# A planner rule that mixes FFN products into attention, with junk products ahead of it, in a fused mLSTM and two-FFN kernel

## The chip, the cores and the metric

The kernel runs on one NeuronCore of a Trainium2 chip. The metric is the device time of one execution in microseconds (us). TensorE (PE in the profile) multiplies, VectorE (DVE), ScalarE (ACT) and GpSimd (POOL) do the elementwise work, and SyncE (SP) issues the DMA transfers.

## What is computed

A recurrent attention with gates (an mLSTM) over 4 batches, 8 heads, 768 steps and 40 values per head, and behind it two feed-forward networks (FFNs) on the 3072 x 320 result:

```python
for t in range(S):                                   # per batch and head
    m_new = np.maximum(f_gate[t] + m, i_gate[t])
    f_stab, i_stab = np.exp(f_gate[t] + m - m_new), np.exp(i_gate[t] - m_new)
    C = f_stab * C + i_stab * outer(v[t], k[t]);  n = f_stab * n + i_stab * k[t]
    y[t] = sigmoid(o_gate[t]) * (C @ q[t]) / np.maximum(abs(n @ q[t]), 1.0);  m = m_new
x = y.transpose(0, 2, 1, 3).reshape(B * S, H * D)
x = np.maximum(np.maximum(x @ w1, x @ w2), x @ w3) @ w_out        # 320 -> 768 -> 320
h = x @ w_in                                                      # 320 -> 2048
out = (h * np.clip(h + 3.0, 0.0, 6.0) / 6.0) @ w_out2             # 2048 -> 320
```

## The kernel before

The recurrence is cut into 6 chunks of 128 steps. A group `g` (0 to 23) is one chunk of one batch, with its 8 heads; it is written out in `attention(g)`. Within a group TensorE runs these steps, each of 8 to 16 or 32 small instructions: `bc` (lines 407 to 412, groups 0 to 3 only) broadcasts a gate row; `sc` (450, two steps a group) multiplies keys and queries; `in` (471) multiplies queries with the state of the chunk before; `pv` (484) sums the values; `dc` (547) makes the new state; `tr` (521) transposes the result for the FFN. `gps` (310) transposes gate values. In the first two chunks (groups 0 to 7) `sc` and `in` multiply on 40 rows in f32, later on 120 rows in a split format. DVE, ACT and POOL work between these steps: a decay scan and a product for `fd`, sums, a reciprocal, the sigmoid.

The first FFN takes blocks of 2, 2, 4, 4, 4, 4 and 4 groups (`BLK1`), so its products are 256 columns wide for two blocks and 512 later. A step `h` (`f_in`, line 630) is 8 products of one of six slices `k` with one of three weights; ACT or DVE takes the running maximum `m`; ACT and POOL split it into `hh`; a step `acc` (`f_out`, line 663) is 5 or 3 products that sum the outputs over the slices. Each of the 24 weight tiles arrives as raw 64-bit data and passes through ACT, DVE, ACT (line 609) and POOL in `weights(k, p)`. The second FFN (from line 763; `pi`, `po`) follows in the same way and is not touched.

What runs when on each engine in the first part is written out by a planner, `class Plan`. Every step is entered by `P.add` with an engine, a cost in ns, a priority `pr` (lower comes first; attention has 1000 times its group, FFN products 10**6 and more), what it reads and writes, and so its buffers (`BUFS`: three PSUM buffers `pa` for `sc`, `in`, `pv`, `dc`, `tr`, `gps`; two `h`; and so on). Steps of FFN products carry the tag `ffn`. `order()` is a list scheduler: in each round it works out for every ready step the earliest start `s` (its engine, its inputs with a latency, a free buffer), and takes the step with the smallest key; so the earliest start wins, and the priority decides between equal starts. The loop at line 748 then issues the steps in the planned order of start; each engine keeps that order. Where the plan leaves TensorE over 600 ns without work, the loop puts in products of constant data (`wps`, line 751), counted at 430 ns each on a running clock `t_pe`, until the first step that uses the PSUM buffer `acc2`, which `wps` shares.

Of the kernel before, what the change touches and what calls it, by code (L numbers as in the profile page):

```python
# [33 lines left out]
JOIN, LAG1 = 4, 3  # L34
BLK2 = [4] * 6
LAG, PIB = 3, 5
SLOPE = 0.0
AHEAD, WPR = 5, 100
GPB, GGB = 3, 4
PE_, PM, PC = 0, 2 * 10**6, 3 * 10**6  # L40
NM1, NM2 = max(BLK1) * L, max(BLK2) * L
# [36 lines left out]
class Plan:  # L78
# [22 lines left out]
    def order(p):  # L101
        free = {t: [0.0] * b for t, b in BUFS.items()}
        left = {s: len(u) for s, u in p.users.items()}
        ends = {s: 0.0 for s in p.users}
        live, done = set(), {}
        at = dict.fromkeys(("PE", "DVE", "ACT", "POOL", "SP"), 0.0)
        dma = 0.0
        todo = {o["n"]: len(o["deps"]) for o in p.ops}
        after = {}
        for o in p.ops:  # L110
            for d in o["deps"]:
                after.setdefault(d, []).append(o["n"])
        ready = {n for n, k in todo.items() if k == 0}
        res = []
        while ready:
            best = None
            for n in ready:
                o = p.ops[n]
                s = at[o["eng"]]
                for d in o["deps"]:  # L120
                    x = p.ops[d]
                    end = done[d]
                    if x["eng"] != o["eng"] or x["eng"] == "SP":
                        end += p.LAT.get(x["eng"], 0) + o["wait"]
                    s = max(s, end)
                ok = True
                for t in o["slots"] - live:
                    if not free[t[0]]:
                        ok = False
                        break  # L130
                    s = max(s, min(free[t[0]]) + 100)
                if ok:
                    e = at[o["eng"]]
                    s = max(s, e)
                    key = (s + SLOPE * min(o["pr"], 20000), o["pr"], n, s)
                    if best is None or key < best:
                        best = key
            assert best, "no buffer for any step"
            _, _, n, s = best
            o = p.ops[n]  # L140
            ready.discard(n)
            for t in o["slots"] - live:
                free[t[0]].remove(min(free[t[0]]))
                live.add(t)
            o["at"] = s
            at[o["eng"]] = s + o["ns"]
            end = s + o["ns"]
            if o["eng"] == "SP":
                dma = max(dma, s) + o["size"] / 210
                end = dma + 2000  # L150
            done[n] = end
            for t in o["slots"]:
                left[t] -= 1
                ends[t] = max(ends[t], end)
                if left[t] == 0:
                    free[t[0]].append(ends[t])
            res.append(o)
            for m in after.get(n, ()):
                todo[m] -= 1
                if todo[m] == 0:  # L160
                    ready.add(m)
        assert len(res) == len(p.ops), "a step never comes"
        p.end = max(done.values())
        return sorted(res, key=lambda o: (o["at"], o["n"]))


def body(tc, ctx, qk0, qkf, kvo, ig, fg, w1, w2, out):
    nc = tc.nc
# [14 lines left out]
    def prio(p):  # L183
        tc.cur_priority = p
# [39 lines left out]
    def products(ps, wt, hi, lo, x):  # L224
        order = [(hi, 0), (hi + 128, 1), (lo, 0), (hi, 3), (lo + 128, 1), (hi + 128, 4), (hi + 256, 2), (lo + 256, 2)]
        for n, (a, r) in enumerate(order):
            nc.tensor.matmul(ps, wt[:, a:a + 128], x[:, r], start=n == 0, stop=n == len(order) - 1)  # L227
# [5 lines left out]
    with ExitStack() as c1:  # L233
# [3 lines left out]
        late = {}  # L237
# [12 lines left out]
        junk = cs1.tile([128, 512], BF16, name="junk")  # L250
# [485 lines left out]
        for seq, (what, j, k) in enumerate(order1()):  # L736
# [3 lines left out]
            else:  # L740
                f_out(j, k, 4 * seq)
        order = P.order()
        n_gates = max(n for n, o in enumerate(order) if o["tags"] & {"gf", "gi", "gm"})

        wps = psh.tile([128, 512], F32, tag="acc2", name="wps")
        t_pe, fill = 500.0, True
        with tc.manual_schedule():
            for n, o in enumerate(order):
                if o["eng"] == "PE" and fill:
                    while n and t_pe + 600 < o["at"]:  # L750
                        nc.tensor.matmul(wps, junk[:, 0:128], junk, start=True, stop=True)  # L751
                        t_pe += 430
                    t_pe = max(t_pe, o["at"]) + o["ns"]
                if n == n_gates + 1:
                    gp1.__exit__(None, None, None)
                    late["hp"] = c1.enter_context(pool("hp"))
                if "acc2" in o["tags"]:
                    fill = False
                prio(10 * n)
                o["fn"]()  # L760


    with ExitStack() as c2:
# [131 lines left out]
def build(arrays):  # L895
    nc = bacc.Bacc("TRN2", target_bir_lowering=False, num_devices=1)
    args = {
        n: nc.dram_tensor(f"in_{n}", a.shape, mybir.dt.from_np(a.dtype), kind="ExternalInput").ap()
        for n, a in arrays.items()
    }  # L900
    out = nc.dram_tensor("out_0", (B * S, DM), F32, kind="ExternalOutput").ap()
    with tile.TileContext(nc, schedule_with_timeline_sim=True) as tc, ExitStack() as ctx:
        body(tc, ctx, out=out, **args)
    return nc
# [9 lines left out]
```

## Time and profile before

| | us |
|---|---|
| median of 3 runs | 808.36 (807.01 to 811.66) |
| the profiled execution | 809.83 |
| its span, first to last instruction | 808.1 |
| TensorE busy | 792.9 (98%) |
| POOL, DVE, ACT busy | 372.3, 351.3, 308.9 |

The table is read from the top: the metric, then the one execution that the profile shows, then the share of its span in which each engine worked. The busy time counts an engine at work and says nothing of its speed. TensorE's clock has two levels, and the profile gives the granted clock beside the busy times, as a part of full speed.

### The profile page before, as it was taken

The numbers are of one execution on the slowest core, as the hardware profiler recorded it, in microseconds if no ns is written. First come the engines' busy times: TensorE is split into PE (matmuls) and PEld (weight loads), VectorE is DVE, ScalarE is ACT, GpSimd is POOL, SyncE is SP. The second block draws the span as 40 slices with busy tenths as digits, with TensorE's granted clock in tenths as the row PEclk, the third lists the DMA queues.
The fourth block names the chain that finished last, engine by engine and source line by source line (L and its number), as shares of the span: only waits on it lengthen the run. The fifth ranks groups of instructions, "written<-read, shape, count | busy, mean of one in ns | idle before, by whom it ended". The sixth has DMA issues, their size and how long they took to land.

```text
span 808.1 us, 12015 instructions
## 1 busy us (share of the span) xinstructions
PE 792.9 (98%) x4583; PEld 698.7 (86%) x4585; DVE 351.3 (43%) x562; ACT 308.9 (38%) x594; POOL 372.3 (46%) x338
## 2 busy tenths in 40 slices
PE   9999999999999998999999999999999999999997
PEld 7789999988888786888788888899898988989886
DVE  5658555766557454564423666321212212121110
ACT  2645351213222221321422889443434333443432
POOL 2557664664756544432411556533534434343332
PEclk7557788999999998999999999999999999999999
DMA  7677576766776736841421454100200000000000
GB/s 221 119 212 259 185 242 178 192 185 171 215 229 212 222 117 176 219 171 49 133 66 34 151 176 136 51 16 1 66 1 1 33 1 1 34 1 1 33 1 33
DMA packets 48974, 91.77 MB, mean 114 GB/s; under 512 B 5740, under 2 KB 25748, under 8 KB 48596
## 3 DMA queue, kind: packets, MB, share of 16 engines
q1 hardware_dynamic: 48916, 91.00, 38.3%
q8 instruction: 36, 0.59, 0.3%
q14 instruction: 22, 0.18, 0.1%
HBM read 70.81 MB, written 18.45 MB: 110 GB/s over the span
## 4 chain that ended last, share of the span: by engine, by line
PE 85%; ACT 5%; POOL 3%; DVE 3%; DMA 2%; issue 1%; SPq 1%; ACTq 0%; POOLq 0%
PE h L227 22%; PE pi L227 19%; PE po L836 6%; PE po L835 6%; PE po L837 6%; PE pv L487 6%; PE sc L453 5%; PE acc L674 5%; PE in L474 3%; PE dc L550 2%; PE acc L676 2%; PE bc L412 1%; DVE t L210 1%; DMA qs<-qs_d 1%; PE wps L751 1%
## 5 line engine op out<-in xcount | busy, mean ns | idle before, releaser
L227 PE MATMUL h<-x,w 128*128 128x512 f32 (+1 forms) x1008 | 227.9, 380 | 1.1 <-ACT m L642 1.1
L821 POOL TENSOR_TENSOR gg<-r,gg 128x512 fp32r<-128x512 f32 x96 | 125.6, 1317 | 183.5 <-ACT gg L820 173.4
L227 PEld LDWEIGHTS h<-x,w 128*128 128x128 f32 x1008 | 180.3, 205 | 31.7 <-ACT m L642 2.5
L227 PE MATMUL pi<-xs,w 128*128 128x512 f32 x768 | 193.3, 395 | 1.5 <-ACT w L779 0.8
L227 PEld LDWEIGHTS pi<-xs,w 128*128 128x128 f32 x768 | 140.8, 188 | 29.7 <-ACT w L779 1.1
L818 DVE SCALAR_TENSOR_TENSOR r<-r,pi 128x512 f32<-128x512 f32 x96 | 64.3, 686 | 229.4 <-ACT r L817 229.2
L835 PE MATMUL po<-w,gg 128*128 128x320 f32 x384 | 118.2, 310 | 0.5 <-DVE x L704 0.2
L836 PE MATMUL po<-w,gg 128*128 128x320 f32 x384 | 118.0, 309 | 0.0
L817 ACT ACTIVATE r<-pi,b 128x512 f32<-128x512 f32 x96 | 63.8, 685 | 133.9 <-PE pi L227 133.3
L837 PE MATMUL po<-w,gg 128*128 128x320 f32 x384 | 111.2, 309 | 0.0
L658 POOL TENSOR_TENSOR hh<-m,hh 128x512 fp32r<-128x512 f32 (+1 forms) x42 | 51.1, 1217 | 89.3 <-ACT hh L654 80.0
L644 DVE TENSOR_TENSOR m<-h,m 128x512 f32<-128x512 f32 (+1 forms) x84 | 51.4, 612 | 87.4 <-PE h L227 82.7
L835 PEld LDWEIGHTS po<-w,gg 128*128 128x128 f32 x384 | 72.1, 188 | 4.8 <-ACT gg L820 0.6
L674 PE MATMUL acc<-hh,w 128*128 128x512 f32 (+1 forms) x252 | 75.1, 376 | 0.0
L836 PEld LDWEIGHTS po<-w,gg 128*128 128x128 f32 x384 | 72.1, 188 | 3.1
L820 ACT CAST gg<-r 128x512 fp32r<-128x512 f32 x96 | 59.0, 621 | 36.6 <-DVE r L818 34.4
L654 ACT CAST hh<-m 128x512 fp32r<-128x512 f32 (+1 forms) x42 | 23.5, 559 | 128.5 <-PE acc L674 124.6
L837 PEld LDWEIGHTS po<-w,gg 128*128 128x128 f32 x384 | 70.4, 188 | 0.9
L217 POOL TENSOR_TENSOR w<-t,w 128x384 fp32r<-128x384 f32 (+2 forms) x46 | 43.6, 961 | 27.2 <-ACT w L609 15.4
L427 DVE TENSOR_TENSOR_SCAN fd<-fd,ident 128x512 f32<-128x512 f32 x40 | 51.6, 1297 | 2.8 <-DMA fd<-f_d 2.7
L674 PEld LDWEIGHTS acc<-hh,w 128*128 128x128 f32 x252 | 46.1, 195 | 6.9
L487 PEld LDWEIGHTS pv<-vt,fd 128*128 128x128 f32 x384 | 50.5, 209 | 1.4 <-issue 0.4
(83 smaller groups left out, 859.2 us busy)
## 6 DMA issues: line engine op xcount, KB each, us to landing
raw<-in_w SPq DMA_DIRECT2D x34, 384.0 KB
kvo<-in_kvo SPq DMA_DIRECT2D x24, 488.0 KB
fd<-f_d SPq DMA_DIRECT2D x20, 512.0 KB
qs_d<-sp SPq DMA_DIRECT2D x16, 640.0 KB
qs<-qs_d SPq DMA_DIRECT2D x64, 160.0 KB
raw<-in_w SPq DMA_DIRECT2D x22, 320.0 KB
raw<-in_qkf SPq DMA_DIRECT2D x16, 320.0 KB
qs<-qs_d SPq DMA_DIRECT2D x16, 320.0 KB
```

The lines of the kernel that those rows point to most:

```text
L227: nc.tensor.matmul(ps, wt[:, a:a + 128], x[:, r], start=n == 0, stop=n == len(order) - 1)
L427: nc.vector.tensor_tensor_scan(out=half, data0=s.get(("bc", a), half), data1=ident4.rearrange("p h t -> p (h t)"), initial=0.0, op0=ALU.mu ...
L487: nc.tensor.matmul(ps[:, h], s["fd"][:, h], s["vt"][:, h], start=True, stop=True)
L644: nc.vector.tensor_tensor(out=T["m", j, k], in0=T["h", j, k, w], in1=T["m", j, k], op=ALU.max)
L674: nc.tensor.matmul(acc[a], wo[:, a * 128:128 + a * 128], h, start=first, stop=last)
L817: nc.scalar.activation(r, ps, AF.Relu, bias=b3)
L818: nc.vector.scalar_tensor_tensor(out=r, in0=r, scalar=6.0, in1=ps, op0=ALU.min, op1=ALU.mult)
L820: nc.scalar.copy(gg[:, 0], r)
L821: nc.gpsimd.tensor_tensor(out=gg[:, 1], in0=r, in1=gg[:, 0].bitcast(F32), op=ALU.subtract)
L835: nc.tensor.matmul(po[t], hi, wo[:, 0:320], start=first, stop=False)
L836: nc.tensor.matmul(po[t], hi, wo[:, 320:640], start=False, stop=False)
L837: nc.tensor.matmul(po[t], lo, wo[:, 0:320], start=False, stop=last)
```

## The change

A constant `RUN = 1000, 800` is added and `SLOPE`, which was 0.0, goes. In the planner, `low` counts the ns of TensorE steps planned since the last one that was tagged `ffn`. While it is over 1000, the key of every TensorE step without that tag is its start plus 800 ns. The start itself is not changed. Each kind of buffer gets a ranked list of its users (by the priority of the first step that uses each), and where only one buffer of a kind is free, no step gets it but the one whose tile is first in rank. In the loop that issues the steps, each TensorE step is followed by round(ns/900) products of constant data, 128 x 512 in bf16, counted at 215 ns each on `t_pe`; and filling ends at the first step that carries `acc2` or `ffn`.

```diff
-SLOPE = 0.0
+RUN = 1000, 800
...
+        live, done, rank = set(), {}, {}
+        for t, u in p.users.items():
+            rank.setdefault(t[0], []).append(((p.ops[min(u)]["pr"], min(u)), t))
+        for x in rank.values():
+            x.sort()
...
                 for t in o["slots"] - live:
-                    if not free[t[0]]:
+                    if not free[t[0]] or len(free[t[0]]) == 1 and t != rank[t[0]][0][1]:
                         ok = False
                         break
...
-                    key = (s + SLOPE * min(o["pr"], 20000), o["pr"], n, s)
+                    late = RUN[1] if o["eng"] == "PE" and "ffn" not in o["tags"] and low > RUN[0] else 0
+                    key = (s + late, o["pr"], n, s)
...
                 live.add(t)
+                rank[t[0]] = [x for x in rank[t[0]] if x[1] != t]
+            if o["eng"] == "PE":
+                low = 0.0 if "ffn" in o["tags"] else low + o["ns"]
...
-                if "acc2" in o["tags"]:
+                if o["tags"] & {"acc2", "ffn"}:
                     fill = False
                 prio(10 * n)
                 o["fn"]()
+                if o["eng"] == "PE" and fill:
+                    for _ in range(round(o["ns"] / 900)):
+                        nc.tensor.matmul(wps, junk[:, 0:128], junk, start=True, stop=True)
+                        t_pe += 215
```

## Rows read from the trace of the kernel before

**Rows 1.** Page, part 1: busy us, share of span, instructions of each engine.
```profile
PE 792.9 (98%) x4583; PEld 698.7 (86%) x4585; DVE 351.3 (43%) x562; ACT 308.9 (38%) x594; POOL 372.3 (46%) x338
```

**Rows 2.** Page, part 2: granted TensorE clock in 40 slices, tenths.
```profile
PEclk7557788999999998999999999999999999999999
```

**Rows 3.** Windows: length, busy us (count) by engine, clock, DMA, GB/s.
```profile
9.10:33.00 23.90, 23.57 (x116) 19.43 (x116) 15.74 (x23) 10.22 (x20) 8.96 (x12) 0.50 0.66 191
33.00:52.30 19.30, 19.08 (x106) 17.06 (x107) 8.66 (x20) 11.64 (x30) 8.68 (x12) 0.59 0.87 183
52.30:141.00 88.70, 88.45 (x641) 84.92 (x641) 54.45 (x100) 37.22 (x87) 55.85 (x64) 0.78 0.67 211
141.00:300.00 159.00, 157.44 (x1040) 137.31 (x1040) 97.95 (x164) 40.37 (x79) 91.49 (x87) 1.00 0.66 194
300.00:341.00 41.00, 37.58 (x201) 31.43 (x200) 19.38 (x32) 9.11 (x17) 20.18 (x18) 0.92 0.74 196
```

**Rows 4.** TensorE groups up to 52.3 us: count | busy us, mean ns.
```profile
L453 PE MATMUL sc<-qs 40*128 40x128 f32 x56 | 13.3, 427 | 0.0
L412 PE MATMUL bc<-gf,ident 32*128 32x128 f32 x64 | 13.2, 373 | 0.3 <-DVE fd L427 0.3
L487 PE MATMUL pv<-vt,fd 128*128 128x42 f32 x48 | 9.3, 375 | 0.0
...
L550 PE MATMUL dc<-vw,kvo 128*40 128x42 f32 x48 | 4.0, 276 | 0.0
...
L314 PE MATMUL gps<-ident,gi 32*128 32x32 f32 x6 | 1.3, 240 | 0.0
```

**Rows 5.** TensorE's timeline, first stretch: start us, us, operation, instructions.
```profile
15.78 3.64 PE L487 MATMUL pv<-vt,fd 128*128 128x42 f32 x16
19.35 3.78 PE L453 MATMUL sc<-qs 40*128 40x128 f32 x16
...
28.44 4.47 PE L751 MATMUL wps<-junk 128*128 128x512 bf16 x10 [0.33 <-issue]
```

**Rows 6.** Timeline, the same kinds of product later.
```profile
119.57 1.07 PE L227 MATMUL h<-x,w 128*128 128x256 f32 x8
...
139.53 1.87 PE L487 MATMUL pv<-vt,fd 128*128 128x42 f32 x16
```

**Rows 7.** Windows before and after the clock's fall at 73.9 us.
```profile
63.70:73.90 10.20, 10.20 (x105) 9.74 (x106) 7.42 (x15) 6.52 (x16) 6.91 (x7) 1.00 0.83 289
73.90:87.60 13.70, 13.70 (x60) 12.80 (x60) 9.93 (x14) 6.57 (x16) 11.08 (x12) 0.50 0.81 257
```

**Rows 8.** Timeline: the row ending in this fall, FFN product behind.
```profile
67.83 2.05 PE L453 MATMUL sc<-qs 40*128 40x128 f32 x16
...
70.56 1.98 PE L474 MATMUL in<-cn,qs 40*128 40x42 f32 x16
...
72.85 2.56 PE L487 MATMUL pv<-vt,fd 128*128 128x42 f32 x16
75.20 2.05 PE L227 MATMUL h<-x,w 128*128 128x256 f32 x8
```

**Rows 9.** Timeline: first and last of an attention row after 141 us.
```profile
245.09 0.97 PE L474 MATMUL in<-cs,qs 120*128 120x42 f32 x8
...
247.79 1.43 PE L550 MATMUL dc<-vw,kvo 128*40 128x42 f32 x32
```

**Rows 10.** Timeline, TensorE's longest wait.
```profile
311.15 1.94 PE L453 MATMUL sc<-qs 120*128 120x128 f32 x8 [3.15 <-DMA qs<-qs_d]
```

**Rows 11.** TensorE's waits for FFN buffers: us in total, times, longest.
```profile
PE h L227 <- ACT m L642: 1.1, 2, 0.7
```

**Rows 12.** Line 609, weight casts: count, durations, first and last start.
```profile
L609 ACT CAST w<-t x24: 445/512/525, 19.8 to 109.2; 128x384 fp32r<-128x384 f32 x18, 128x320 fp32r<-128x320 f32 x6
```

**Rows 13.** Timeline: last attention product, and FFN products behind it.
```profile
382.48 0.49 PE L524 MATMUL tr<-ident,y 128*128 128x128 f32 x3
...
418.48 5.66 PE L227 MATMUL h<-x,w 128*128 128x512 f32 x24
```

More of the change, by code (lines that the diff above doesn't have):

```diff
@@ L104, in order @@
         ends = {s: 0.0 for s in p.users}
-        live, done = set(), {}
+        live, done, rank = set(), {}, {}
[3 more added lines that the diff above has]
+            x.sort()
         at = dict.fromkeys(("PE", "DVE", "ACT", "POOL", "SP"), 0.0)
-        dma = 0.0
+        dma = low = 0.0
         todo = {o["n"]: len(o["deps"]) for o in p.ops}
```

## The prediction

> **What bounds the kernel now.** I read the busy shares first. TensorE is busy 792.9 of 808.1 us [rows 1], and no other engine reaches half: what ends last is TensorE's own stream, so a change pays only if it shortens that stream. The share hides one thing, which stands a few lines below it on the page: the granted clock, at half in early slices and full from about 140 us on [rows 2]. The windows by stage put numbers on it [rows 3]. From 9.1 to 33 us TensorE is busy 23.57 of 23.90 us at a clock of 0.50, to 52.3 us 19.08 of 19.30 at 0.59, to 141 us 88.45 of 88.70 at 0.78; from 141 to 300 the clock is 1.00. As the clock has two levels (1.2 and 2.4 GHz), a mean of 0.78 over 88.7 us is 2 x 0.22 x 88.7 = 39.0 us at half. In the same way the first two stretches hold 23.9 + 15.8 = 39.7 us, and the 41 us from 300 on (0.92) 6.6 us. Some 85 us run at half clock, and they are the reserve that this change can touch.
>
> What the same product costs at each level is in the timeline. A `pv` step takes 3.64 us early and 1.87 at full clock, a pair of `sc` steps 3.78 and 2.05, eight `h` products of 256 columns 2.05 and 1.07 [rows 5, 6, 8]. A step at full clock takes about 0.55 of its time at half, so a microsecond at half gives back at most 0.45 us. All of it together: 85.3 x 0.45 = 38 us.
>
> What TensorE did before the clock fell: from 67.83 to 75.20 us it ran only attention products (`sc`, `dc`, `in`, `tr`, `pv`), 7.4 us in a row [rows 8], and the clock, full to 73.9, is at half from there to 87.6 [rows 7]. Three more such rows, of 4.5, 4.4 and 4.0 us, end in a fall between 89 and 127 us. After 141 us, where FFN products are mostly 512 columns wide and `in` and `sc` work on 120 rows in place of 40, even a row of 4.1 us (`in`, `pv`, `dc`) costs no clock [rows 3, 9]. TensorE was busy throughout in all of these, so it is which products run that decides here, not idleness.
>
> The Trainium skill ("TensorE: Matmul & The Clock Gate", section "Why this matters for your kernels") advises to keep TensorE busy continuously and to avoid idle gaps between bursts of matmuls, so that the clock stays up. The trace disagrees for these small products: 23.57 of 23.90 us busy, clock 0.50 [rows 3]. The rule speaks against the change, and its result is told with the rivals.
>
> **Part 1, junk products between the first attention steps.** Ahead of the first FFN product at 52.3 us there are 64 `bc` instructions, which are 8 steps, 56 `sc` (7 steps), 48 `pv` (3), 48 `dc` (3) and 6 `gps` steps, one for each transpose of `gi` [rows 4]. With round(ns/900) junk products after each: `bc` 1 (1000 ns), `gps` 1 (500), `sc` 2 (1720), `pv` 2 (1800), `dc` 1 (690), `tr` 0 (340). That is 8 + 6 + 14 + 6 + 3 = 37 new junk products. At half clock one takes 4.47/10 = 0.447 us [rows 5], so 37 take 16.5 us; at full clock I halve that, 8.2 us. Against it, the planner's clock `t_pe` now runs ahead by 215 ns for each, so that most gap fillers of before (the 10 at 28.44 us and 2 shortly before the first `h`, 12 x 0.447 = 5.4 us) are no longer issued. The net work added is +2.8 us at full clock and +11.1 us at half, all of it on the path: TensorE has only 0.55 us of idle time there to hide it in.
>
> What it may buy: of the 39.7 us at half 5.4 are fillers; the 34.3 us of products give back 34.3 x 0.45 = 15.4 us if the clock is held throughout, 2.8 - 15.4 = -12.6 us in all. But DVE, busy 15.74 + 8.66 = 24.40 of 43.20 us there [rows 3], then has the same work in some 30 us, and the fillers stood where TensorE had nothing to do: waits come in, and I take -8 us as this end. At the other end the junk itself runs at half clock and lifts nothing, +11 us. The nearest rows stand on both sides: ten junk products in one piece at 28.44 us were followed by a short full stretch (0.59 after 33 us), and 7.4 us without a wide product ended in a fall [rows 3, 5, 8]. Now the junk comes singly or in pairs, at full clock 0.45 us of it after 1.05 us of `sc` or 1.87 us of `pv`, and 0.22 us after a `bc`: a fifth to a third of the time. For such a mix the trace has no row. I take the middle of -8 and +11, rounded down: +1 us.
>
> **Part 2, the planner breaks up rows of small products.** After over 1000 ns of attention products an FFN product wins if it could start at most 800 ns later. By the planner's costs a row is cut after each `sc` and `in` of the first eight groups, after `pv`, and after `dc` with `tr`; from group 8 on after two `sc` and an `in`. At full clock the longest row is then about `dc` and `pv`, 0.8 + 1.9 = 2.7 us, shorter than each of the four that ended in a fall. The FFN products brought forward cost nothing in sum: it is the same work, issued earlier. Of the 39.0 us at half, 8 lie ahead of 64 us, around the first FFN products, where rows are short already; I leave them. The other 31 us give back 31 x 0.45 = 14 us if all go. I take about two thirds, -9 us, for two reasons. FFN steps of the first two blocks need weights that are made until 109 us [rows 12], so some rows find none to put in. And the rule also breaks up runs of FFN products: eight `h` products alone at half clock (75.20 us) didn't bring the clock back before 87.6 [rows 7, 8], so a fall that does come lasts longer. Bounds: -17.6 us (39.0 x 0.45) and, on the other side, +3 us, if single FFN products at half clock leave it down some 7 us longer (7 x 0.45).
>
> What is queued behind: an attention step waits for an FFN step of 1.0 to 1.9 us, some 70 times; DVE, ACT and POOL get `sc`, `pv` and `dc` later, and SP's loads of `qs`, `kvo` and `fd`, which wait for buffers, start later. In the stretch to 141 us DVE is busy 54.45 and POOL 55.85 of 88.70 us [rows 3], so they follow. The last attention product is at 382.48 us; from there to 458 us only FFN products run, of which the last block must come after it: 6 x 5.66 us of `h` and 48 `acc` products at 5.66/24 = 0.24, 45 us [rows 13]. Attention can end 30 us later for nothing.
>
> TensorE may also wait for an FFN product while an attention product is ready. `h` waited for its PSUM buffer twice in the whole kernel, 1.1 us together [rows 11]; I take +1 us, bounds 0 and +4.
>
> **Part 3, last buffer kept for the first in rank.** It puts off a later group's step while an earlier one's has no buffer. Of three `pa` buffers, two stay for `sc`, `pv` and `dc` while one waits for `tr`; each is emptied by a short DVE or ACT step that lies under the next TensorE step. I take nothing, bounds -1 and +3 us. `SLOPE` was 0.0: taking it out does nothing.
>
> **The stall at 308 us.** `sc` waits 3.15 us there for `qs` [rows 10], and 6.6 us at half clock go with it: 3.15 + 6.6 x 0.45 = 6.1 us. SP's queue is put in a new order there, so this can vanish or come twice: 0, bounds -6 and +6.
>
> **Sum.** +1 - 9 + 1 + 0 + 0 = -7 us on the profiled execution's 809.8 us (its span of 808.1 and what lies around it): 802.8. That execution lies 1.5 us above the median of 808.36 (three runs from 807.01 to 811.66), so I predict 801.
>
> **Rivals.** (a) The junk holds the clock from the start, and part 2 finds it up: -8 - 11 + 1 = -18 us, 790. For it: `sc` with its pair of junk has the densest mix; against it: `bc`, with one, comes first. Chance 0.27. (b) Slower: the mix does not lift the clock. 37 junk products run at 0.447 us, and behind them single FFN products of 256 columns at half clock lift it late: +11 - 3 + 1 = +9 us, 817. It decides if the clock falls at about 9 us and isn't back before the first FFN product. For it: from 9 to 33 us nothing lifted the clock but fillers in one piece, and these are taken away. Chance 0.23. (c) The change doesn't do what it says: FFN steps aren't ready within 800 ns, rows stay as they are, and the junk about pays for itself: +1 us, 809. Against it: FFN products run between attention rows already [rows 6, 8]. Chance 0.07. (d) What the clock follows is only whether TensorE is busy: then neither part lifts anything and the junk is pure cost, 809.8 + 11 + 1, about 820 as a median. The busy share at half clock [rows 3] contradicts it; 0.03. This is what the skill's rule told above would give. The forecast keeps 0.40.
>
> **How the numbers follow.** The measurement of this kernel can tell about 0.5%, 4 us, from no change. Faster by more: nearly all of (a) and three quarters of the forecast, 0.56. Within it: a fifth of the forecast, most of (c) and the near edge of (b), 0.18. Slower: most of (b), (d) and the tails, 0.26. The forecast's own range is 793 to 810; to hold the time 8 times in 10 the range takes in (a) with its bound and (b): 786 to 818.
>
> **What would show it.** Right: a clock over 0.9 from 65 to 141 us with no attention row over 3 us, and some 37 more `wps` products before the first `h`, with fewer in one piece. The first `h` starts near 53 us in the forecast, near 44 in (a), near 63 in (b). Wrong: a clock still under 0.8 from 65 to 141 us although the rows are cut; new TensorE waits for `h` buffers or for `qs` that sum to over 5 us; or an attention end so late that TensorE idles ahead of the second network.

## The result, and the profile after

| | before | after |
|---|---|---|
| median of 20 executions each, us | 808.9 (802.62 to 817.15) | 816.14 (808.83 to 826.45) |
| ratio | | 1.0091, 95% interval 1.0062 to 1.0119 |
| the profiled execution, its span, us | 809.83, 808.1 | 819.8, 818.1 |
| TensorE busy, us | 792.9 (98%) | 802.9 (98%) |

The changed kernel is 0.9% slower; the prediction was 801 us, faster. In all comparisons below the ratio and its interval count the executions that lie within 1.5% of the fastest of their kernel, and the ratio of the means of all executions stands beside them where more than one is left out, since a kernel that spreads by itself looks better without its slow ones.

The granted clock in 40 slices of the changed kernel's span, from its page; it answers [rows 2]:

```profile
PEclk7555978999999999999999999999999999999999
```

The windows of the changed kernel, with the bounds and columns of [rows 3]:

```profile
9.10:33.00 23.90, 23.23 (x107) 16.81 (x108) 11.79 (x18) 5.89 (x14) 5.00 (x6) 0.50 0.46 138
33.00:52.30 19.30, 18.83 (x72) 13.56 (x73) 7.04 (x14) 10.60 (x25) 8.33 (x11) 0.50 0.67 119
52.30:141.00 88.70, 86.27 (x566) 78.27 (x567) 53.63 (x94) 39.56 (x92) 55.63 (x60) 0.74 0.64 200
...
300.00:341.00 41.00, 39.73 (x227) 33.72 (x226) 22.53 (x36) 10.96 (x20) 18.93 (x18) 1.00 0.79 225
```

Until 52.3 us the clock is now at half without a break (0.50 and 0.50, where it was 0.50 and 0.59), to 141 us it is lower than before (0.74 against 0.78), and the fall behind 300 us is gone. The same execution, cut where the clock changes:

```profile
9.10:66.30 57.20, 54.99 (x235) 40.03 (x239) 22.30 (x36) 19.95 (x47) 16.73 (x22) 0.50 0.57 145
66.30:80.60 14.30, 14.25 (x62) 13.50 (x63) 9.68 (x17) 6.20 (x15) 8.32 (x10) 0.50 0.26 80
80.60:111.20 30.60, 29.29 (x261) 27.22 (x260) 22.80 (x40) 20.50 (x48) 26.93 (x29) 1.00 0.76 245
111.20:128.30 17.10, 17.10 (x84) 15.81 (x84) 9.25 (x16) 5.91 (x13) 9.41 (x11) 0.50 0.61 197
```

There are two half-clock stretches: one from 8.9 to 80.5 us, and one from 111.3 to 128.3. In between the clock is full for 30.6 us. TensorE's timeline of the changed kernel shows what runs in the first stretch, and how it ends:

```profile
10.27 0.61 PE L773 MATMUL wps<-junk 128*128 128x512 bf16 x1
10.81 2.07 PE L463 MATMUL sc<-qs 40*128 40x128 f32 x8
12.81 1.04 PE L773 MATMUL wps<-junk 128*128 128x512 bf16 x2
...
66.35 2.07 PE L237 MATMUL h<-x,w 128*128 128x256 f32 x8 [0.57 <-ACT x L540]
68.36 2.07 PE L463 MATMUL sc<-qs 40*128 40x128 f32 x8
...
75.93 2.08 PE L237 MATMUL h<-x,w 128*128 128x256 f32 x8
...
78.30 3.13 PE L237 MATMUL h<-x,w 128*128 128x256 f32 x16
81.36 1.16 PE L463 MATMUL sc<-qs 40*128 40x128 f32 x8
```

The junk stands singly and in pairs between the attention steps, and eight `sc` products still take 2.07 us. The first `h` starts at 66.35 us; before, it started at 52.36. Single `h` steps follow at half clock (2.07 us for 8 products), and only the first two that stand together, at 78.30, end at full clock.

Where the 14.0 us ahead of the first `h` come from is in the groups of TensorE up to it. The changed kernel:

```profile
L773 PE MATMUL wps<-junk 128*128 128x512 bf16 x30 | 16.8, 595 | 1.2 <-issue 1.2
L422 PE MATMUL bc<-gf,ident 32*128 32x128 f32 x64 | 14.6, 396 | 0.0
...
L497 PE MATMUL pv<-vt,fd 128*128 128x42 f32 x48 | 10.4, 410 | 0.0
L761 PE MATMUL wps<-junk 128*128 128x512 bf16 x10 | 4.7, 631 | 1.5 <-DVE gm L278 1.5
```

The same view of the kernel before, up to its first `h`, for the group that isn't among [rows 4]:

```profile
L751 PE MATMUL wps<-junk 128*128 128x512 bf16 x20 | 9.1, 633 | 2.1 <-DVE gm L268 1.5 <-issue 0.6
```

Junk takes 16.8 + 4.7 = 21.5 us in place of 9.1: +12.4 us. This is most of it. (The program issues 45 junk products ahead of the first `h` in place of 22: 35 new ones, since one `sc` step with its pair now comes behind the first `h`, less 12 fillers. A few records are missing.) The same 64 `bc` and 48 `pv` cost 14.6 and 10.4 us in place of 13.2 and 9.3 [rows 4], since the short full-clock stretch of before is gone. TensorE also stands idle 1.4 us longer up to there (3.8 us in place of 2.4), and does one `sc` step less.

Since that `sc` step (2.07 us) now comes behind it, the first `h` isn't the same point in both kernels. An estimate at equal work: add up TensorE's products other than junk, each at the spacing that it has at full clock, and compare when the two traces reach the same sum. By this count the changed kernel lags by 15.9 us where the kernel before starts its first `h`, by 14.7 at its 141 us, 15.2 at 305, 8.9 at 341, and 10.0 at the end, the difference of the spans. So almost nothing is won to 141 us (1.2 us); 6.3 us are won at 308 us, where the wait of 3.15 us [rows 10] and the half clock behind it are gone; and 1.3 us are lost at 414 us, where `h` waits 1.75 us for `m`.

### The profile page after: what moved, and what is told of

Read it like the earlier page. It is cut to its first block, busy times and chain, and to the rows that moved or that the text cites. A ratio compares the mean times of both kernels' runs of the same rounds, so it can differ in the third digit from the quotient of the medians.

```text
span 818.1 us, 12055 instructions
## 1 busy us (share of the span) xinstructions
PE 802.9 (98%) x4603; PEld 697.6 (85%) x4608; DVE 358.9 (44%) x562; ACT 308.6 (38%) x594; POOL 370.0 (45%) x338
## 4 chain that ended last, share of the span: by engine, by line
PE 86%; ACT 5%; DVE 3%; DMA 2%; POOL 2%; SPq 1%; issue 1%; ACTq 0%
PE h L237 22%; PE pi L237 19%; PE po L850 6%; PE po L849 6%; PE po L851 6%; PE pv L497 6%; PE acc L684 5%; PE sc L463 5%; PE in L484 3%; PE dc L560 2%; PE wps L773 2%; PE bc L422 2%; DVE t L220 2%; PE acc L686 2%; DMA qs<-qs_d 1%
## 5 line engine op out<-in xcount | busy, mean ns | idle before, releaser
L237 PE MATMUL h<-x,w 128*128 128x512 f32 (+1 forms) x1008 | 222.9, 372 | 2.3 <-ACT m L652 1.7
L237 PEld LDWEIGHTS h<-x,w 128*128 128x128 f32 x1008 | 174.1, 196 | 32.9 <-ACT m L652 3.1
L668 POOL TENSOR_TENSOR hh<-m,hh 128x512 fp32r<-128x512 f32 (+1 forms) x42 | 53.6, 1276 | 91.7 <-ACT hh L664 79.0
L437 DVE TENSOR_TENSOR_SCAN fd<-fd,ident 128x512 f32<-128x512 f32 x40 | 54.9, 1381 | 3.0 <-DMA fd<-f_d 2.9
L497 PEld LDWEIGHTS pv<-vt,fd 128*128 128x128 f32 x384 | 52.5, 215 | 1.1
L497 PE MATMUL pv<-vt,fd 128*128 128x42 f32 x384 | 51.7, 301 | 0.0
```

The lines of the kernel that those rows point to most:

```text
L437: nc.vector.tensor_tensor_scan(out=half, data0=s.get(("bc", a), half), data1=ident4.rearrange("p h t -> p (h t)"), initial=0.0, op0=ALU.mu ...
L497: nc.tensor.matmul(ps[:, h], s["fd"][:, h], s["vt"][:, h], start=True, stop=True)
L668: nc.gpsimd.tensor_tensor(out=t[:, 1], in0=T["m", j, k], in1=t[:, 0].bitcast(F32), op=ALU.subtract)
```

## The experiments

Each run is compared with the kernel before on its own chip. "All" is the ratio of the means of all executions, with more than one left out of the interval.

| | edit | median, us | ratio, 95% interval (counted of all) | all | first `h`, us |
|---|---|---|---|---|---|
| | the change | 816.14 | 1.0091, 1.0062 to 1.0119 (15 of 20) | 1.011 | 66.35 |
| e1 | junk alone | 827.76 | 1.0227, 1.0178 to 1.0276 (6 of 6) | | 70.86 |
| e2 | planner parts alone | 801.09 | 0.9887, 0.9836 to 0.9938 (6 of 6) | | 50.23 |
| e3 | late rule alone | 802.35 | 0.9900, 0.9848 to 0.9951 (6 of 6) | | 52.16 |
| e4 | last-buffer rule alone | 803.68 | 0.9926, 0.9895 to 0.9956 (12 of 12) | | 54.30 |
| e5 | junk alone, tripled | 811.10 | 0.9970, 0.9929 to 1.0011 (7 of 10) | 1.002 | 65.42 |
| e6 | planner parts, FFN steps in pairs | 796.83 | 0.9824, 0.9774 to 0.9873 (6 of 6) | | 50.28 |
| e7 | before, third `fd` buffer | 806.76 | 0.9952, 0.9915 to 0.9989 (12 of 12) | | 49.82 |
| e8 | planner parts, third `fd` buffer | 809.08 | 0.9958, 0.9923 to 0.9993 (8 of 12) | 0.999 | 50.86 |
| e9 | change, junk tripled | 804.49 | 0.9823, 0.9758 to 0.9888 (4 of 6) | 0.991 | 53.63 |
| e10 | change, FFN steps in pairs | 809.87 | 1.0011, 0.9976 to 1.0047 (11 of 12) | | 69.04 |
| e11 | change, fillers kept | 807.91 | 0.9928, 0.9884 to 0.9971 (9 of 12) | 0.997 | 58.16 |
| e12 | planner parts, FFN steps in threes | 797.12 | 0.9829, 0.9789 to 0.9868 (6 of 6) | | 50.27 |
| e13 | change, junk tripled at `bc` | 814.70 | 0.9983, 0.9941 to 1.0024 (5 of 12) | 1.010 | 75.14 |
| e14 | change, piece of 12 ahead of `sc` | 810.48 | 0.9954, 0.9909 to 0.9998 (8 of 12) | 0.997 | 59.90 |
| e15 | change, fillers kept, pairs | 798.67 | 0.9875, 0.9828 to 0.9921 (5 of 6) | | 63.25 |
| e16 | change, junk tripled, pairs | 798.71 | 0.9843, 0.9767 to 0.9920 (5 of 6) | | 60.86 |

The first `h` is that of one profiled execution, which can lie several us from the others of its kernel; the profiles of e5, e13 and e15 are of executions that the ratio doesn't count.

**The parts alone (e1 to e4).** The late rule is the 800 ns that the key adds; the rank rule keeps the last free buffer for the first in rank. e1 is the change without its late rule and its rank rule; e2 without its junk; e3 without junk and rank rule; e4 without junk and with a late rule of 0 ns.

e1 (its second edit is in e3 as well):

```diff
-late = RUN[1] if o["eng"] == "PE" and "ffn" not in o["tags"] and low > RUN[0] else 0
+late = 0
...
-if not free[t[0]] or len(free[t[0]]) == 1 and t != rank[t[0]][0][1]:
+if not free[t[0]]:
```

e2, and with it e3 and e4:

```diff
-if o["eng"] == "PE" and fill:
-    for _ in range(round(o["ns"] / 900)):
-        nc.tensor.matmul(wps, junk[:, 0:128], junk, start=True, stop=True)
-        t_pe += 215
```

e4:

```diff
-RUN = 1000, 800
+RUN = 1000, 0
```

> The kernel before with the junk products between the first attention steps and nothing else of the change (planner key and buffer rule as before). Theory J (the junk runs at half clock and lifts nothing, so it is added work on the path): the first h starts near 66 us instead of 52, the clock is 0.50 from 9 to 52 us, and the median is 12 to 15 us above before, ratio 1.015 to 1.019. Theory P (the planner's two rules make the loss, the junk pays for itself): ratio 0.997 to 1.003.

> The changed kernel without the junk products; both planner rules stay. Theory J: the 14 us lag of the first h is gone and the change's other parts remain, so 3 to 8 us below before, ratio 0.990 to 0.996. Theory P: slower than before by most of the change's loss, ratio 1.006 to 1.012.

> Of the change only the rule that delays small products by 800 ns in the key after 1000 ns; no junk, buffers as before. Theory J: at or below before, ratio 0.990 to 1.000; rows of attention products over 4 us are gone from 52 to 141 us. Theory P: 1.004 to 1.012, as single FFN products at half clock leave the clock down longer than before (over 45 us at half between 52 and 141 us, 39 before).

> Of the change only the rule that keeps the last free buffer for the first in rank. The prediction took nothing for it: ratio 0.997 to 1.003. If the vanished stall at 308 us came from this rule, there is no wait of sc for qs over 1 us and the ratio is 0.990 to 0.995; if the rule holds TensorE up, there are new idle stretches that sum to over 3 us and the ratio is above 1.004.

The junk alone costs 2.3%, 18.4 us; the planner parts alone gain 1.1%, 9.2 us; their sum, +9.2, is near the change's +7.4 (0.0091 x 808.9). So the loss is the junk's. In e1 the clock did not rise ahead of the first `h` at all: its timeline (junk alone) has the first and the last `sc` at the same length.

```profile
13.45 2.07 PE L463 MATMUL sc<-qs 40*128 40x128 f32 x8
...
68.38 2.07 PE L463 MATMUL sc<-qs 40*128 40x128 f32 x8
...
70.86 3.98 PE L237 MATMUL h<-x,w 128*128 128x256 f32 x16
```

The late rule and the rank rule gain about as much each alone (8.1 and 6.0 us) as together (9.2), so their gains don't add up. The profiles say why. With either rule alone the wait for `qs` at 308 us and its fall are gone; the windows of e3 (first line) and e4:

```profile
300.00:341.00 41.00, 41.00 (x236) 34.91 (x234) 24.32 (x38) 11.88 (x23) 21.61 (x18) 1.00 0.73 214
300.00:341.00 41.00, 41.00 (x226) 35.17 (x225) 22.02 (x39) 11.01 (x22) 19.31 (x19) 1.00 0.77 223
```

At equal work, counted as above, 6.0 us of e3's gain and 6.3 of e4's lie there, and 1.1 and 2.3 us between the first `h` and 141 us. With both rules it is the other way round; the windows of e2 (planner parts alone):

```profile
52.30:141.00 88.70, 88.70 (x729) 83.98 (x728) 66.70 (x114) 40.89 (x95) 66.91 (x72) 0.91 0.76 234
141.00:300.00 159.00, 157.31 (x974) 134.74 (x974) 95.00 (x151) 37.43 (x73) 84.52 (x84) 0.96 0.71 195
```

To 141 us 2 x 0.09 x 88.7 = 16.0 us are at half, where it was 39.0 [rows 3], and at equal work e2 has won 9.0 us there. There a stall stands in another place: `sc` waits 1.69 us at 285 us, for what the profile doesn't name, and 2 x 0.04 x 159 = 12.7 us are at half, where it was none. So in the profiles each rule alone gains mostly by the order of the loads, and the two together by TensorE's clock ahead of 141 us.

**What the stall at 308 us costs (e7, e8).** A third buffer is meant to let the load for `fd` be issued without waiting, so that it no longer holds up the loads of `qs` in SP's queue. The same table enters the plan, so the order of the steps changes with it.

```diff
-    qs=2, raw=1, sp=1, kvo=2, fd=2, vt=2, ...
+    qs=2, raw=1, sp=1, kvo=2, fd=3, vt=2, ...
```

> The kernel before with one edit: three fd buffers in place of two, so that SP's load for fd no longer waits for a buffer ahead of the loads of qs in its queue. Theory Q (the stall at 308 us and the half clock behind it cost 6.1 us, and most of what the late rule or the rank rule gain alone is that this stall goes away): the sc there starts without the 3.15 us wait, the clock from 300 to 341 us is 1.00, ratio about 0.992, some 804 us. Rival T (the two rules gain by the clock ahead of 141 us, and the stall is worth little or only moves): ratio 0.998 to 1.002.

> The planner parts without junk, and three fd buffers. In the planner parts alone a wait of 1.7 us for qs at 285 us and 13.7 us at half clock behind it remain, which are worth 1.7 + 13.7 x 0.45 = 7.9 us. Theory Q (the load for fd that waits for its buffer holds up the loads of qs): this goes, and the time falls from 801 to some 794. Rival T (the wait has another cause, or a new one takes its place): 801 within 2 us.

In e7 the wait is gone; TensorE's timeline goes from `h` to `sc` without one.

```profile
301.38 1.99 PE L227 MATMUL h<-x,w 128*128 128x512 f32 x8
303.31 1.08 PE L453 MATMUL sc<-qs 120*128 120x128 f32 x8
```

e7 is 0.5% faster (0.1 to 0.85%), 3.9 us, under the 6.1 of theory Q but with that in its interval. Not all of it is the stall: in its profile, which is its fastest execution, 6.1 us are won at the stall and 5.0 by 141 us, in another order of the steps. With the planner parts the third buffer gained nothing: e8 is at 0.9958 against e2's 0.9887. There `sc` waits 2.83 us for `qs` at 203 us, and the clock from 66 to 141 us is 0.77. So theory Q fits e7 and fails as a rule for this queue. That the load for `fd` holds up those of `qs` is not shown: each edit here made a new plan, and a new plan can lose the wait (e3, e4, e7) or bring another (e2, e8).

**Whether more junk lifts the clock (e5).**

```diff
-for _ in range(round(o["ns"] / 900)):
+for _ in range(round(o["ns"] / 300)):
```

> The junk part alone as in the first experiment, but round(ns/300) junk products after each TensorE step in place of round(ns/900): 112 wps products ahead of the first h in place of 47. Theory J (in such a mix junk does not lift the clock, whatever the dose): 65 more products at 0.447 us are 29 us of pure cost, first h near 100 us, some 857 us. Rival D (the dose was too small, and enough junk does lift the clock): from 9 us on the products of the first experiment (about 45 us at half clock) take 25 us and some 97 junk products at 0.22 us take 21 us, so the first h is near 56 us, sc steps of 8 take 1.1 us in place of 2.07, and the time is some 812 us. A mixed outcome (it lifts late) lies between.

Theory J falls here: the loss isn't that junk never lifts the clock. With 112 junk products in place of 47 the time came down from 1.0227 to 0.9970. The timeline of e5 shows it: eight `sc` products take 2.08 us at 21 us and 1.16 from 32 us on, behind pieces of six junk products.

```profile
18.45 2.74 PE L773 MATMUL wps<-junk 128*128 128x512 bf16 x6
21.12 2.08 PE L463 MATMUL sc<-qs 40*128 40x128 f32 x8
23.13 2.74 PE L773 MATMUL wps<-junk 128*128 128x512 bf16 x6
...
32.38 1.16 PE L463 MATMUL sc<-qs 40*128 40x128 f32 x8
...
65.42 2.23 PE L237 MATMUL h<-x,w 128*128 128x256 f32 x16
```

The first `h` is at 65.42 us all the same, since the junk itself takes time at full clock too. Even this dose pays for itself at most.

**What the missing piece was worth (e11, e14, e13).** In the change the running clock `t_pe` counts the junk, so the fillers in one piece are no longer issued. e11 leaves the junk uncounted, which brings them back (11 near 38 us and 4 ahead of the first `h`, where the change has 2); e14 puts a piece of 12 ahead of the first `sc`; e13 puts three junk products in place of one behind each `bc`.

e11:

```diff
                         nc.tensor.matmul(wps, junk[:, 0:128], junk, start=True, stop=True)
-                        t_pe += 215
```

e14:

```diff
-        t_pe, fill = 500.0, True
+        t_pe, fill, piece = 500.0, True, False
...
                 prio(10 * n)
+                if not piece and o["ns"] == 1720:
+                    piece = True
+                    for _ in range(12):
+                        nc.tensor.matmul(wps, junk[:, 0:128], junk, start=True, stop=True)
+                        t_pe += 215
                 o["fn"]()
```

e13:

```diff
-for _ in range(round(o["ns"] / 900)):
+for _ in range(round(o["ns"] / (300 if o["ns"] == 1000 else 900))):
```

> The change with one edit: the junk products after each step are not counted on the clock t_pe, so that the fillers in one piece are issued as before (11 at about 29 us and 4 ahead of the first h, 13 more than in the change). Theory F (a piece lifts the clock for one short stretch, and singles and pairs behind it don't hold it): 13 x 0.447 = 5.8 us of cost against some 3 us that the stretch gives back, ratio 1.010 to 1.015. Rival H (singles and pairs can't lift a clock, but hold one that a piece has lifted): clock full from 33 us to the first h, which comes some 33 x 0.45 - 4 = 11 us earlier than in the change, near 55 us; ratio 0.995.

> The change with one edit: 12 junk products in one piece ahead of the first sc (at 11 us), 57 wps products ahead of the first h in place of 45. Theory H (a piece lifts the clock, singles and pairs hold it from there): the piece takes some 4.5 us, the clock is full by 16 us, and from there to the first h the products take 0.55 of their time: 66 + 4.5 - 50 x 0.45 = about 48 us for the first h, some 800 us, ratio 0.988. Rival G (the mix of sc, dc, bc and pv with singles and pairs lets it fall again, as it did behind the first 8 junk products at 5 us): 816 + 5 - 3, ratio 1.010 to 1.014, first h at 68 us.

> The change with one edit: three junk products in place of one behind each of the 8 bc steps, 61 wps products ahead of the first h in place of 45. Theory H (singles and pairs hold a clock that is up; the fall at 8.9 us comes from the thin mix at bc): the clock stays full from 5 us on, 16 x 0.22 = 3.5 us more junk, sc steps of 8 at 1.16 us from the first, first h at 45 to 50 us in place of 66, some 798 us, ratio 0.985. Rival G (the clock falls in the sc rows anyway, or isn't up at 5 us in some executions): 16 x 0.447 = +7 us at half, ratio 1.012 to 1.018, with first h at 70 us.

e11 is the decisive run: 13 junk products more, and 1.6% less time than the change (0.9928 against 1.0091; by all executions 1.4%, 0.997 against 1.011). Its timeline, the change with the fillers kept:

```profile
28.48 2.07 PE L463 MATMUL sc<-qs 40*128 40x128 f32 x8
...
38.21 1.49 PE L761 MATMUL wps<-junk 128*128 128x512 bf16 x3
39.91 2.82 PE L761 MATMUL wps<-junk 128*128 128x512 bf16 x7 [0.22 <-issue]
...
49.33 1.16 PE L463 MATMUL sc<-qs 40*128 40x128 f32 x8 [0.25 <-issue]
50.42 0.61 PE L773 MATMUL wps<-junk 128*128 128x512 bf16 x2
...
58.16 1.31 PE L237 MATMUL h<-x,w 128*128 128x256 f32 x8
```

And its windows behind the piece, up to the first `h` and on to 141 us:

```profile
43.00:58.10 15.10, 14.79 (x112) 11.14 (x113) 6.41 (x12) 9.97 (x27) 6.65 (x9) 1.00 0.74 157
58.10:141.00 82.90, 82.82 (x719) 77.99 (x718) 70.17 (x121) 40.93 (x97) 66.60 (x70) 0.98 0.79 246
```

Up to the piece the mix of singles and pairs is at half clock as in the change; behind it the same mix runs at full clock, and the single FFN steps find the clock up and keep it but for 2 x 0.02 x 82.9 = 3 us. (This execution, at 800.63 us, is near the fastest of e11, which run from 799.86 to 817.09: the profile shows the mechanism at its best.) e14 says the same with a piece at another place: from 15.5 to 32.6 us its clock is 0.98, and `sc` takes 1.16 us. Then it falls again and stays down to the first `h`; the windows of e14:

```profile
15.50:32.60 17.10, 15.01 (x119) 11.29 (x121) 12.27 (x20) 8.88 (x17) 3.72 (x5) 0.98 0.44 128
32.60:59.90 27.30, 26.18 (x109) 18.99 (x110) 9.18 (x16) 10.71 (x30) 11.82 (x16) 0.50 0.79 160
```

Where it falls, TensorE had caught up with the gates' work on DVE and waited 1.58 us for `gm`; the timeline of e14:

```profile
32.39 0.31 PE L324 MATMUL gps<-ident,gm 32*128 32x32 f32 x1 [1.58 <-DVE gm L299]
```

In e11 it is at this place that the fillers stand. Even there the mix gains nothing over leaving it out: e2, with the fillers and without the mix, is at 0.9887 against 0.9928. So behind such a piece the mix keeps a lifted clock for a time and not for good: 17 us here, and 10 us in the profile of e15, which has the same products as e11 up to the first `h` and falls in a row without a wait of over 0.3 us. Without the mix, the clock that the fillers lift at 31 to 35 us is full for 3 to 7 us (the kernel before, e2, e3, e4, e6, e7, e8, e12). The mix doesn't always do that much: behind the first eight fillers, at 5 us, the clock was down by 9 us in the change, e11, e14 and e15, as it was without the mix in the kernel before.

e13 did not do what was expected of it: in its profiled execution the clock was already down at 5.2 us (`bc` at 2.04 us), three junk products behind `bc` did not bring it back, and the first `h` came at 75.14. Its executions run from 801 to 841 us, and by all of them it is as slow as the change. Theory H holds as far as "a piece lifts, singles and pairs don't". That the thin mix at `bc` is what lets the clock fall at 8.9 us isn't settled by e13; e9 speaks for it, with three junk products behind each `bc` and six behind each `sc`: its profile starts with the clock up (`bc` at 1.15 us from 5.05 on) and keeps it to 94 us.

**Single FFN steps (e6, e12, e10, e9, e15, e16).** The count of small products goes back to 0 only after 1800 ns of FFN products, so that two 256-column steps stand together (2800 in e12: three). e6 and e12 have no junk, e10, e15 and e16 have it as the change, e11 and e5. e9 is the change with round(ns/300).

```diff
-        dma = low = 0.0
+        dma = low = wide = 0.0
...
-                low = 0.0 if "ffn" in o["tags"] else low + o["ns"]
+                wide = wide + o["ns"] if "ffn" in o["tags"] else 0.0
+                low = low + o["ns"] if not wide else 0.0 if wide >= 1800 else low
```

> The planner parts without junk, with one edit: the count of small products is set back to 0 only after 1800 ns of FFN products in a row, so that while FFN products are 256 columns wide (about 1000 ns a step) two stand together in each break. Theory S (a single FFN step of 8 products at half clock does not lift it, a longer piece does): the half-clock time from 52 to 141 us, 15 us with single steps, falls to some 8 us, and the time goes from 801 to some 797. Rival R (only the length of the attention row counts): half-clock time and time as with single steps, 801, within 2 us, or a little slower, as the FFN products of ready weights run out sooner.

> The planner parts without junk, with three FFN steps in each break (the count goes back to 0 only after 2800 ns of FFN products). Theory S (the longer the piece of FFN products, the surer the clock lifts): ratio at or below that of pairs, 0.980 to 0.983. Rival E (the FFN steps whose weights are there run out, and the rows of attention products behind them grow to 10 us and more): a fall in such a row between 95 and 125 us, ratio 0.988 to 0.995.

> The change with one edit: the count of small products goes back to 0 only after 1800 ns of FFN products in a row, so that two steps stand together in each break; the junk stays as in the change. Theory S (behind the junk, a single FFN step at half clock lifts it late, and pairs lift it at once): of the 14 us at half behind the first h and the 17 us from 111 us on, most goes, 31 x 0.45 = 14 us at most; I expect two thirds of it, 807 us, ratio 0.998. Rival R (what is lost is lost ahead of the first h): the ratio stays at 1.006 to 1.012.

> The change with one edit: round(ns/300) junk products in place of round(ns/900), 110 wps products ahead of the first h in place of 45. The triple dose alone lifted the clock at 26 us and held it up to the first h at 65 us, at a ratio of 0.997. Theory W (a single FFN step in each break holds a clock that is up; it fails only where it has to lift one that is down): first h near 62 us, clock over 0.95 from 66 to 141 us, 811 - (13 to 14 us at half clock there x 2 x 0.45 = 12) = some 798 us, ratio 0.985. Rival S (single FFN steps of 8 products don't hold it either): falls between 66 and 141 us as with the triple dose alone, ratio 0.997 less what the stall is worth, 0.990 to 0.997.

> The change with the fillers in one piece kept (as in e11) and two FFN steps in each break. Theory S (single FFN steps of 8 products also let the clock fall again behind the first h, pairs don't): ratio 0.993 less the 0.6 to 0.8% that pairs gave in the two comparisons without and with junk, 0.985 to 0.987. Rival W (with the clock up at the first h, single steps hold it as well as pairs): 0.991 to 0.995.

> The change with two edits: round(ns/300) junk products in place of round(ns/900), and the count of small products goes back to 0 only after 1800 ns of FFN products. Theory S (single FFN steps are a second cause: behind a wait they let the clock fall, at 94 us in the run with the triple dose, 27 us at half clock in all): most of that goes, 27 x 0.45 = 12 us at most and 6 us taken, ratio 0.975 against 0.982. Rival W (once the clock is full at the first h, pairs give nothing more): 0.980 to 0.985.

e10 against the change: 1.0011 against 1.0091, intervals apart, although its first `h` is no earlier. Its timeline shows the clock back by the end of the first pair, where the change needed 14 us:

```profile
69.04 3.58 PE L238 MATMUL h<-x,w 128*128 128x256 f32 x16 [0.57 <-ACT x L541]
72.55 1.16 PE L464 MATMUL sc<-qs 40*128 40x128 f32 x8
73.64 2.15 PE L238 MATMUL h<-x,w 128*128 128x256 f32 x16
```

At the first `h` the same contrast stands without junk. The timeline of e2, single steps, is at half clock for nearly 14 us:

```profile
50.23 2.27 PE L237 MATMUL h<-x,w 128*128 128x256 f32 x8
52.43 2.07 PE L463 MATMUL sc<-qs 40*128 40x128 f32 x8
...
62.37 2.85 PE L237 MATMUL h<-x,w 128*128 128x256 f32 x16
```

The timeline of e6, pairs:

```profile
50.28 3.45 PE L238 MATMUL h<-x,w 128*128 128x256 f32 x16
53.66 1.16 PE L464 MATMUL sc<-qs 40*128 40x128 f32 x8
```

The other profiles with the clock down at the first `h` agree: with single steps it came up after 11 to 14 us in five (the change, e2, e8, e13, e14) and after 3 us in e3, to fall once more; with 16 products or more in a row it came up after 2 to 5 us in eight (the kernel before, e1, e4, e6, e7, e10, e12, e15). A pair is no certainty. In the kernel before a later one lifted nothing; its timeline:

```profile
79.19 3.78 PE L227 MATMUL h<-x,w 128*128 128x256 f32 x16
82.90 2.07 PE L453 MATMUL sc<-qs 40*128 40x128 f32 x8
```

And what pairs gain in time without junk (e6 against e2, 0.6%, intervals overlapping) isn't this in the profiles: from 52.3 to 141 us the clock of e6 is 0.92 against e2's 0.91, where theory S had the half-clock time fall by half, and at equal work e2 has won 9.0 us there and e6 7.3. e6 is ahead because it has no such stall as e2 behind.

Where the clock is up at the first `h`, pairs make no difference that these runs show: e16 against e9 is 0.9843 against 0.9823. e15 against e11, 0.9875 against 0.9928 with overlapping intervals, is no clean test, as the clock of e15's profile was down again at its first `h`. So theory S is right for a clock that is down (e10), and rival W can't be told from it for one that is up. In e9 the clock does fall with single steps, at 94 us, behind a wait of 1.33 us for `vw`; e16's profile has one fall of 3.4 us. Threes (e12) are no better and no worse than pairs. e6 is 1.8% faster than the kernel before, and among the fastest of all versions here; it has no added junk.

## Why the prediction was wrong

**The bound** was read rightly: the reserve is the half-clock time, and every version that gained did so by that and by the stalls behind 141 us. (The 0.45 us given back for a microsecond at half is a little low: `pv` goes from 3.64 to 1.87 us, 0.49.)

**Part 1 is the step that failed first.** The step reads "I take the middle of -8 and +11, rounded down: +1 us". In the profile after the first `h` is 14.0 us late, 15.9 at equal work, and by the ratios the junk costs (1.0091 - 0.9887) x 809 = 16.5 us. The upper end was sized nearly right for what it counted, +12.4 us of junk against the +11.1 worked out. (A single at half clock takes 0.54 us from its start to that of the next step and a pair 0.97, somewhat over 0.447 each; 35 new ones and 12 fillers less are close to the 37 and 12 of the step.) Two things in the step were wrong:
- The price of the fillers that go. They were booked as 5.4 us saved. I had the row of ten fillers in one piece with a full stretch behind it [rows 3, 5], and used it as evidence that the mix might lift the clock; but the mix replaces that very piece. e11 puts the price on it: with the piece back, 0.9928 in place of 1.0091, 13 us (12 by all executions), although it and the two fillers ahead of the first `h` are themselves 6 us of work.
- "For such a mix the trace has no row", and so the middle. The mix does two different things, and a middle between ends fits neither: from a clock that is down it never lifted it, for 57 us in the change, 64 in e10 and 66 in e1; a clock that a piece of ten or more had lifted it held for 10 us, 17 us, or up to the first `h` (e15, e14, e11), and behind the first eight fillers for no longer than without the mix.

**Rival (b)** named the mechanism: the mix doesn't lift the clock, and single FFN products lift it late; it gave 817 us and a first `h` near 63 us, where 816.14 and 66.35 were measured. Its condition, the clock down from about 9 us and not back before the first FFN product, is what the profile shows. That the figure came so near is luck in part: of its terms, +11 measured about 16, and the stall at 308 us, not among them, took 6 off. I gave it 0.23 and the forecast 0.40; since all that spoke for (b) was in the rows (nothing from 9 to 33 us lifts the clock but fillers in one piece, and these go), it should have had more. Rival (d) gives about the same time for another reason, and e11 rules it out: TensorE was busy 14.79 of 15.10 us at full clock there, and 23.57 of 23.90 at half in [rows 3].

**Part 2.** For the planner parts alone the -9 us came out (e2: -9.2), in the profile for the reason given: 9.0 us won to 141 us, with 16.0 us at half in place of 39.0. In the changed kernel this step failed too: there the rule won 1.2 us at equal work. Behind the first `h` 14.2 and 17.1 us are at half, 31.3 in all against 38.6 in the kernel before, which is worth 7.3 x 0.45 = 3.3 us, and waits take part of it back (1.3 us for `vw`). From 65 to 141 us the clock is 0.79 although the rows are cut, which the prediction had named as a sign of being wrong. The step reckoned with a clock that the cut rows would hold; Part 1 left it down, and single FFN steps took 14 us to lift it, where the bound of +3 us allowed for 7. Pairs in their place gain 0.8%, 6.5 us (e10).

**The smaller terms.** Waiting for an FFN product: `h` waited once for `m`, 1.7 us, at 414 us, where it was 1.1 in all before [rows 11], within the 0 to +4. The stall at 308 us went away, -6.3 us at equal work, at the edge of -6 to +6; why the new order avoids it wasn't followed. Part 3 at 0 is not refuted by e4's 6.0 us (3.6 to 8.5): in its profile 6.3 us are won at that stall, which has a term of its own, and 2.3 to 141 us, where the clock is 0.83, 30 us at half in place of 39. How much of these 2.3 is the rule's and how much the execution's stays open.

## What to carry to other kernels

Before a change takes away filler work, ask what the filler does to the clock, not only what time it takes: here a piece of eleven junk products bought more than it cost once something behind it held the clock. Tell lifting from holding: what holds a clock that is up need not lift one that is down, and between two such cases no middle should be taken; find the row that says in which of them the stretch starts. And when a scheduler's rule is changed, look at the queue of loads too: two rules that aimed at TensorE gained in their profiles, each alone, most of their time at a DMA wait 250 us further on.

## What the runs showed of the hardware

The clock of a stretch depended on what came before it, with the same products: in e11 singles and pairs between `sc` steps ran at half clock to 38 us (`sc` 2.07 us) and at full clock from 43 us (1.16 us), with one piece of eleven junk products in between.

The clock column can be wrong at the start of an execution. In e3 the window from 9.1 to 33 us shows 1.00, with 120 TensorE products of the kinds that e2 shows at 0.51 (118 products); in e1 the column is 1.00 while `sc` takes 2.07 us. The durations decide.

```profile
9.10:33.00 23.90, 23.90 (x120) 20.60 (x120) 16.45 (x24) 10.23 (x20) 7.09 (x9) 1.00 0.63 179
```

The Trainium skill ("TensorE: Matmul & The Clock Gate", section "Seeing it yourself") warns that the clock's events in a trace are not to be trusted one by one; this agrees with it.

Executions of one kernel differ by more than the effects looked for: 808.83 to 826.45 us after, 802.62 to 817.15 before, 801 to 841 in e13. Where the clock falls and comes back differs from one execution to the next: all 18 profiles begin with the same eight junk products, and behind them the first `bc` step took 1.12 to 1.51 us in eleven and 2.04 to 2.07 in seven. So one profile gives a mechanism and not the size of an effect.
